# The last half tile in two pieces, late stores on ScalarE's queue, and a new order of work

## Chip, cores and metric

The kernel runs on one core of a Trainium2 chip. The metric is the device time of one execution in microseconds (us). A core has TensorE (PE, matrix products, with its weight loads as PEld), VectorE (DVE), ScalarE (ACT), GpSimd (POOL) and SyncE (SP), which here only issues DMAs. Each of the five runs its own list of instructions in order; semaphores join them.

## What is computed

A gate g, one number for each of the 2048 tokens, mixes two attention layers over the same x (640 wide, 32 heads of 20): A is linear attention with softmax feature maps, B is causal attention inside four segments of 512 tokens, with a memory carried from segment to segment.

```python
g = _sigmoid((x * gate_w).sum(-1, keepdims=True))
# A: phi = softmax(+-(q @ w_phi)) and the same for k, 40 wide
kv = einsum('bhsf,bhsd->bhfd', phi_k, v);  z = einsum('bhsf->bhf', phi_k)
a = (einsum('bhqf,bhfd->bhqd', phi_q, kv) / (phi_q . z + 1e-6)) @ wo_A
# B: for each segment s of 4
p = softmax(q_s @ k_s.T * 20**-0.5 + mask)
o = sigmoid(beta) * (phi(q_s) @ M) / (phi(q_s) @ z) + (1 - sigmoid(beta)) * (p @ v_s)
M += phi(k_s).T @ v_s;  z += phi(k_s).sum()
b = o @ wo_B
return g * a + (1 - g) * b
```

## The kernel before

The kernel is a list of 1394 operations, built in `build` (L1019). An operation is one step of one engine (a chain of matmuls, one evacuation, one DMA) with the tiles that it reads and writes. `Graph.replay` then takes three texts that stand in the file: ORDER, the place of every operation in one list (each engine runs its own operations in that order, SP's DMAs too); ENGINE, for the 255 operations that two or three engines could do, which of them does it; and PLACE, the buffer or the PSUM banks of each of the 618 floating tiles. `emit` adds the semaphore waits that follow from the tiles: data, and the reuse of a buffer or bank. At the very end SP waits for every DMA slot whose landing it doesn't know of yet (L253).

The steps that the prediction speaks of, by their lines:

- Setup: weights are loaded and turned or cast (WB, L499, on DVE, ACT or POOL), x is turned on PE (L484), and the first segment is projected (qproj0 L593, kproj0 L604) and copied out as qk (q0_ev, k0_ev). The two weight products with w_phi are made on PE (fuse, L567) and copied out as WkA and WqA. The last of those and all evacuations below go through `evac` (ACT L426 or DVE L427).
- B, for each segment: projections (L613 for q and k, L633 and L634 for v); QK bursts (L730), four heads side by side, into two PSUM tiles of two banks; each tile goes through one exp on ACT (L741, 160 exps of 128x1024 in all), is masked on POOL (L743) and used by the PV step (L773), whose result nT is copied out and written to memory; `b_out` reads it back as nB, divides (nrec L806, nmul L808), and adds the memory's part aT (nadd, L717).
- B's memory: k and q pass through a feature map (pk, pq: L652 to L654), Mmm (L671) and mr (L702) are its products, L708 to L711 its evacuation.
- A: pkA and vA (L818), kexp (L831), sums and scaling (L837 to L841), kv (L861) with its sums (L874, L884); then for each 512 tokens pqA (L931), qexp (L938), ssum (L946), the scaling of half of ET by sp (Esc, L962), and for each tile of 128 tokens U (L976) with its evacuation (L982 to L985).
- The end: `final(t)`, for each of 16 tiles of 128 tokens. Two PE steps (final0 from A's oTA, final1 from B's nB; L1006) add ten products into two PSUM banks of 320 columns; an evacuation scales them by 1-g, and a store writes 128x640. For the last four tiles each half of 320 columns has its own two steps, evacuation and store. All stores of results go through SP.

PE, ACT, DVE and POOL thus work on A, B and final interleaved, as ORDER says. PSUM has 8 banks; S and U and F tiles take two each.

Of the kernel before, what the change touches and what calls it, by code (L numbers as in the profile page):

```python
# [16 lines left out]
NT = 16  # L17
# [244 lines left out]
class GatedMix(Graph):  # L262
# [730 lines left out]
    def final(self, t):  # L993
        pt = self.pst("F", 2)
        ob = self.sbt("out", [128, D], BF16, self.p_out)
        oT, nB, q = self.oTA[t], self.nB[t // 4], t % 4
        parts = ((0,), (1,)) if t >= NT - 4 else ((0, 1),)
        ops = {}
        for bs in parts:
            for k, (lhs, R) in enumerate(((lambda c: oT[:, c, :], [(oT, "*"), (self.Wo, 0)]),  # L1000
                                          (lambda c: nB[:, c, 128 * q:128 * q + 128], [(nB, q)] + [(self.Wo, (1, dd)) for dd in range(4)]))):
                def mm(e, k=k, lhs=lhs, bs=bs):
                    first = ops[bs, k].pos < ops[bs, 1 - k].pos
                    for c in range(NCH):
                        for b in bs:
                            r = e.matmul(self.pf(pt, b, 0, 320), lhsT=lhs(c), rhs=self.Wo[:, NCH * k + c, 320 * b:320 * b + 320],  # L1006
                                         start=(first and c == 0), stop=(not first and c == 4), skip_group_check=True)
                    return r
                ops[bs, k] = self.op("pe", f"final{k}", mm, R=R, W=[(pt, (bs[0], k))])
        out2d = self.out.rearrange("b s d -> (b s) d")  # L1010
        for bs in parts:
            n, c0 = len(bs), 320 * bs[0]
            src = (lambda: self.pbanks(pt, 320)) if n == 2 else (lambda b=bs[0]: self.pf(pt, b, 0, 320))
            dst = (lambda: ob[:, :].rearrange("p (b c) -> p b c", b=2)) if n == 2 else (lambda c0=c0: ob[:, c0:c0 + 320])
            self.evac("out_ev" if n == 2 else "outh_ev", dst, src, R=[(self.omg, t // 4)],
                      W=[(pt, (bs[0], 0)), (pt, (bs[0], 1)), (ob, bs[0])], scale=lambda: self.omg[:, t:t + 1])
            self.dma("sp", "out", out2d[128 * t:128 * (t + 1), c0:c0 + 320 * n], lambda c0=c0, n=n: ob[:, c0:c0 + 320 * n], R=[(ob, bs[0])])
# [140 lines left out]
```

## Time and profile before

| | us |
|---|---|
| median of 3 runs (lowest, highest) | 289.42 (289.36, 290.12) |
| the profiled execution, device time | 288.96 |
| its span, first to last instruction | 287.2 |
| mean granted TensorE clock in it | 1.000 |
| PE, DVE, ACT, POOL busy | 275.4, 224.1, 234.5, 163.7 |

The page gives busy time of each engine, a picture of the span in 40 slices, DMA queues, the chain of waits that ended last, and the costliest groups of instructions. Busy time of PE is that of overlapping matmuls: one of 320 columns is shown with 299 ns, while the next starts 136 ns later. An instruction that waits is not busy; the time is put down to what came last.

### The profile page before, as it was taken

To read this page: it belongs to the slowest core of one execution; us is meant where nothing else is said; L and a number is where in the kernel's file an instruction comes from. 1 tells how busy PE (TensorE), PEld (TensorE's weight loads), DVE (VectorE), ACT (ScalarE), POOL (GpSimd) and SP (SyncE) were. 2 spreads that over 40 slices of the span, in tenths; PEclk is the share of its full clock that TensorE was granted. 3 is DMA by queue.
4 is the path that set the end of the run, shared out by engine and by line. 5 is a ranking of instruction groups with operands and counts; after the bars stand their busy time and mean duration, and the time that the engine had idled before them with its cause. 6 is when DMAs were issued, how large, how long until landed. Compare 5 with 4: busy or idle time off the path is not lost.

```text
span 287.2 us, 7648 instructions
## 1 busy us (share of the span) xinstructions
PE 275.4 (96%) x3155; PEld 162.2 (56%) x3155; DVE 224.1 (78%) x395; ACT 234.5 (82%) x270; POOL 163.7 (57%) x171
## 2 busy tenths in 40 slices
PE   7999999999999899999999999989998999999996
PEld 3755535564356555646754554544465456667774
DVE  3777997856896799988799979787963696788873
ACT  3589999898999998899799999999899988772110
POOL 6421698638869648796794671584955434263030
PEclk9999999999999999999999999999999999999999
DMA  7999400551158046432135664985946596665793
GB/s 227 259 249 227 91 21 18 114 77 37 57 92 126 14 112 132 59 84 75 34 41 103 161 154 101 188 231 121 154 107 160 120 215 184 151 146 145 168 182 113
DMA packets 75212, 36.25 MB, mean 126 GB/s; under 512 B 56458, under 2 KB 73258, under 8 KB 75178
## 3 DMA queue, kind: packets, MB, share of 16 engines
q1 hardware_dynamic: 73872, 34.26, 54.0%
q10 hardware_dynamic: 1242, 1.48, 1.5%
q8 instruction: 25, 0.41, 0.6%
q0 software_dynamic: 64, 0.03, 0.1%
q14 instruction: 9, 0.07, 0.1%
HBM read 13.44 MB, written 11.50 MB: 87 GB/s over the span
## 4 chain that ended last, share of the span: by engine, by line
PE 68%; ACT 18%; DVE 7%; POOL 5%; issue 1%; POOLq 0%
PE ps L1006 14%; PE ps L818 9%; PE ps L613 9%; ACT exA L741 9%; PE ps L730 6%; PE ps L773 5%; PE ps L931 5%; ACT exC L741 4%; PE ps L861 3%; PE ps L976 3%; PE ps L633 3%; PE ps L634 2%; ACT ET L938 2%; DVE z L837 2%; PE ps L604 2%; PE ps L593 2%
## 5 line engine op out<-in xcount | busy, mean ns | idle before, releaser
L741 ACT ACTIVATE exA<-ps 128x1024 bf16<-128x1024 f32 x128 | 123.4, 1034 | 12.4 <-PE ps L730 12.1
L743 POOL TENSOR_SCALAR_AFFINE_SELECT exA<-exA 128x1024 bf16<-128x1024 bf16 (+1 forms) x64 | 58.1, 917 | 55.9 <-ACT exA L741 55.9
L841 POOL TENSOR_TENSOR E<-E,z 128x640 bf16<-128x640 bf16 x26 | 34.2, 1325 | 10.2 <-DVE lc L637 7.6
L613 PE MATMUL ps<-xT,WB 128*128 128x512 bf16 x150 | 37.0, 380 | 1.1 <-ACT exA L741 0.8
L741 ACT ACTIVATE exC<-ps 128x1024 bf16<-128x1024 f32 x32 | 31.0, 1023 | 4.1 <-PE ps L730 3.8
L730 PE MATMUL ps<-qk 20*128 20x128 bf16 (+3 forms) x512 | 31.7, 301 | 1.9 <-ACT exA L741 0.8
L831 ACT ACTIVATE E<-ps,sg 128x640 bf16<-128x640 f32 x32 | 25.3, 803 | 1.0 <-DVE acc L884 0.4
L743 POOL TENSOR_SCALAR_AFFINE_SELECT exC<-exC 128x1024 bf16<-128x1024 bf16 x16 | 18.4, 1153 | 12.3 <-ACT exC L741 12.3
L818 PE MATMUL ps<-WvA,xT 128*128 128x320 bf16 x160 | 24.1, 300 | 0.8 <-ACT exA L741 0.8
L837 DVE TENSOR_REDUCE z<-E 128x64 f32<-128x1280 bf16 x16 | 23.5, 1471 | 1.5 <-ACT E L831 1.4
L931 PE MATMUL ps<-xT,WqA 128*128 128x512 bf16 x100 | 24.1, 380 | 0.5 <-ACT exC L741 0.3
L818 PE MATMUL ps<-WkA,xT 128*128 128x320 bf16 x160 | 24.1, 300 | 0.3 <-ACT exC L741 0.3
L1006 PE MATMUL ps<-Wo,oTA 128*128 128x320 bf16 x160 | 24.4, 299 | 0.0
L1006 PE MATMUL ps<-Wo,nB 128*128 128x320 bf16 x160 | 24.2, 299 | 0.0
L427 DVE CAST nT<-ps 128x512 bf16<-128x512 f32 x25 | 16.6, 682 | 8.8 <-PE ps L773 8.8
L427 DVE CAST qk<-ps 128x1024 bf16<-128x1024 f32 (+1 forms) x17 | 17.4, 1032 | 7.4 <-PE ps L613 5.3
L773 PE MATMUL ps<-exA,v1B 128*32 128x384 bf16 (+2 forms) x384 | 22.7, 311 | 0.2 <-POOL exA L743 0.2
L633 PE MATMUL ps<-WvB,xT 128*128 128x320 bf16 x80 | 22.5, 300 | 0.2
L613 PEld LDWEIGHTS ps<-xT,WB 128*128 128x128 bf16 x150 | 12.9, 98 | 17.3 <-issue 2.7
L884 POOL TENSOR_TENSOR acc<-acc,E 128x640 bf16<-128x640 bf16 x13 | 18.1, 1395 | 7.8 <-DVE acc L884 6.7
L634 PE MATMUL ps<-WvB,xT 128*128 128x321 bf16 x80 | 22.4, 300 | 0.0
L730 PEld LDWEIGHTS ps<-qk 20*128 20x128 bf16 x512 | 9.1, 92 | 23.6 <-issue 7.6
(132 smaller groups left out, 497.4 us busy)
## 6 DMA issues: line engine op xcount, KB each, us to landing
scn<-nT SPq DMA_DIRECT2D x32, 128.0 KB, 1.8
scq<-rr SPq DMA_DIRECT2D x16, 160.0 KB, 3.0
sp<-scq SPq DMA_DIRECT2D x4, 640.0 KB, 4.4
scr<-qk SPq DMA_DIRECT2D x16, 120.0 KB
qk<-scr SPq DMA_DIRECT2D x16, 120.0 KB
nB<-scn SPq DMA_DIRECT2D x12, 160.0 KB, 3.5
out_dram<-out SPq DMA_DIRECT2D x12, 160.0 KB, 2.1
stk<-in_B_wk_dram SPq DMA_DIRECT2D x5, 160.0 KB, 5.1
```

Of the source, the lines that this page charges most:

```text
L427: return e.tensor_scalar(o(), i(), scale(), None, op0=ALU.mult) if scale else e.tensor_copy(o(), i())
L613: r = e.matmul(self.pf(pt, w, 0, LSEG), lhsT=WB[:, w, kc, 128 * c:128 * (c + 1)], rhs=xT[:, kc, LSEG * n:LSEG * (n + 1)], start=(kc == 0), ...
L633: e.matmul(self.pf(pt, 0, 0, 320), lhsT=l, rhs=self.WvB[:, kc, 0:320], start=(kc == 0), stop=(kc == 4))
L730: r = e.matmul(self.pf(pts[i // 2], i % 2, c0, N), lhsT=qk[32 * i:32 * i + DH, g, 1, 128 * j:128 * (j + 1)], rhs=qk[32 * i:32 * i + DH, g, ...
L741: self.op("act", "exp", lambda e, p=p: e.activation(view(p), self.pbanks(pts[p], 512), ACT.Exp, scale=scale), W=[(pts[p], 0), (t, (key, p))])
L743: self.op("pool", "mask" + str(len(pat)), lambda e: e.affine_select(mv(), mv(), pattern=pat, compare_op=ALU.is_ge, fill=0.0, base=0, chann ...
L773: r = e.matmul(self.ps[32 * i:32 * i + 32, 512 * pt.t[0] + 128 * j:512 * pt.t[0] + 512], lhsT=vt[:, v0:v0 + 32], rhs=src(j, i), start=(j = ...
L818: r = e.matmul(self.pf(pt, b, 0, 320), lhsT=l, rhs=W[:, kc, 320 * b:320 * b + 320], start=(kc == 0), stop=(kc == 4))
L837: self.op("dve", "Zred", lambda e: e.tensor_reduce(z[:, :, :].rearrange("p s h -> p (s h)"), E[:, :, :].rearrange("p s (h d) -> p (s h) d" ...
L841: self.op(("pool", "dve"), "Anorm", lambda e, s=s: e.tensor_tensor(Ev(s), Ev(s), z[:, s, :].rearrange("p (h o) -> p h o", o=1).to_broadcas ...
L931: r = e.matmul(self.pf(pt, k, 0, LSEG), lhsT=self.WqA[:, kc, 128 * c:128 * (c + 1)], rhs=xT[:, kc, LSEG * S:LSEG * (S + 1)], start=(kc == ...
L1006: r = e.matmul(self.pf(pt, b, 0, 320), lhsT=lhs(c), rhs=self.Wo[:, NCH * k + c, 320 * b:320 * b + 320], start=(first and c == 0), stop=(no ...
```

## The change

In `final`, the last four tiles (`late`) issue their stores on ACT's queue in place of SP's. The very last tile's second half becomes two pieces of 160 columns with two PE steps, an evacuation and a store each; the second piece has a PSUM tile of one bank of its own. So four operations and one tile are added (1398 and 619). ORDER, ENGINE and PLACE are new texts throughout. 60 of the operations of before that have a choice of engine run on another one.

```diff
-        parts = ((0,), (1,)) if t >= NT - 4 else ((0, 1),)
+        late = t >= NT - 4
+
+        parts = [(pt, (0, 1), 320, 0)] if not late else [(pt, (0,), 320, 0)] + (
+            [(pt, (1,), 320, 320)] if t < NT - 1 else [(pt, (1,), 160, 320), (self.pst("F", 1), (0,), 160, 480)])
...
+        for pt, bs, n, d0 in parts:
...
-                        for b in bs:
-                            r = e.matmul(self.pf(pt, b, 0, 320), lhsT=lhs(c), rhs=self.Wo[:, NCH * k + c, 320 * b:320 * b + 320],
+                        for i, b in enumerate(bs):
+                            r = e.matmul(self.pf(pt, b, 0, n), lhsT=lhs(c), rhs=self.Wo[:, NCH * k + c, d0 + 320 * i:d0 + 320 * i + n],
...
-            self.dma("sp", "out", out2d[128 * t:128 * (t + 1), c0:c0 + 320 * n], lambda c0=c0, n=n: ob[:, c0:c0 + 320 * n], R=[(ob, bs[0])])
+            self.dma("act" if late else "sp", "out", out2d[128 * t:128 * (t + 1), d0:d0 + w], lambda d0=d0, w=w: ob[:, d0:d0 + w], R=[(ob, d0)])
```

The end of ORDER names the last operations. In the numbers of `final(15)` before, 1386 and 1387 are the PE steps of the first half, 1388 and 1389 those of the second, 1390 to 1393 the evacuations and stores. After, 1386 and 1387 are the first half's, 1388 and 1389 the first piece's, 1390 and 1391 the second piece's; 1392 and 1393, 1394 and 1395, 1396 and 1397 are the evacuations and stores of the three.

```diff
-1363 1364 1372 1329 902 1380 1366 1378 1367 1373 1376 1377 1370 1371 1381 1384 1385 914 1374 1375 1353 1365 1368 1369 1387 1379 1382 1383 1386 1390
-1391 1389 1388 1392 1393
+1364 1368 1379 1325 1380 1369 1378 1381 1384 1366 1385 1382 1352 1383 1353 1372 1373 1376 1377 1357 1361 887 1367 1390 914 1370 1371 1374 1375 1391
+1396 1397 1389 1388 1394 1395 1386 1387 1392 1393
```

Operations by engine, where it changed most (before, after): Anorm POOL 26, 21 and DVE 6, 11; chain DVE 18, 15 and POOL 13, 16; WB ACT 5, 8 and DVE 12, 8; q0_ev ACT 1, 4; fuse_ev ACT 3, 5; nT_ev ACT 7, 8; qk_ev ACT 4, 5; vA_ev ACT 6, 5; out_ev ACT 5, 7; nadd POOL 3, 6; nmul POOL 0, 1; Esc of one chunk POOL 0, 3.

## Rows read from the trace of the kernel before

**Rows 1.** The page's busy shares, and its chain of waits by engine.

```profile
PE 275.4 (96%) x3155; PEld 162.2 (56%) x3155; DVE 224.1 (78%) x395; ACT 234.5 (82%) x270; POOL 163.7 (57%) x171
PE 68%; ACT 18%; DVE 7%; POOL 5%; issue 1%; POOLq 0%
```

**Rows 2.** The chain of waits in order of time: start us, us, what.

```profile
71.94 1.08 PE ps L613 x5
...
85.75 2.89 PE ps L818 x20
...
89.92 0.33 PE ps L730 x8
...
101.16 0.66 PE ps L773 x16
...
202.84 1.25 PE ps L931 x5
...
213.18 0.36 PE ps L730 x8
...
215.50 5.50 ACT exA L741 x6
...
252.87 0.80 PE ps L976 x12
...
262.41 0.69 PE ps L976 x12
...
266.90 17.67 PE ps L1006 x130
284.59 0.53 ACT out L426
```

**Rows 3.** The first instructions in order of time: start us, us, engine, line, what.

```profile
0.81 0.41 ACTq L418 DMA_DIRECT2D xn<-in_A_x_dram  x1
0.81 0.39 SPq L418 DMA_DIRECT2D xn<-in_A_x_dram  x1
...
1.26 3.57 PE L466 MATMUL ps<-zero 128*128 128x512 bf16 x8 [1.26 <-DVE sg L514]
```

**Rows 4.** Busy time by stretch: length, then each engine's us (instructions), clock, DMA.

```profile
95.00:102.50 7.50, 6.85 (x154) 4.69 (x155) 6.42 (x11) 7.42 (x9) 3.69 (x4) 1.00 0.18 46
213.30:221.00 7.70, 6.89 (x66) 3.75 (x59) 3.21 (x8) 7.44 (x9) 2.15 (x2) 1.00 0.52 122
...
257.80:284.60 26.80, 26.76 (x264) 19.80 (x260) 19.90 (x41) 4.08 (x8) 5.76 (x5) 1.00 0.68 159
284.60:287.20 2.60, 0.00 (x0) 0.00 (x0) 0.00 (x0) 0.52 (x1) 0.00 (x0) 1.00 0.20 63
```

**Rows 5.** Groups of instructions of the last 33 us: count, busy us, mean ns.

```profile
L1006 PEld LDWEIGHTS ps<-Wo,nB 128*128 128x128 bf16 x90 | 8.6, 98 | 3.4 <-issue 0.2
```

**Rows 6.** The end in order of time, all engines; idle time before in brackets.

```profile
281.95 3.53 SPq L418 DMA_DIRECT2D out_dram<-out  x5
...
284.59 0.53 ACT L426 ACTIVATE out<-ps,omg 128x320 bf16<-128x320 f32 x1 [5.58 <-PE ps L1006]
```

**Rows 7.** DMA issues: count, KB each, median us from issue to landing.

```profile
out_dram<-out SPq DMA_DIRECT2D x8, 80.0 KB, 1.7
```

**Rows 8.** Groups of ACT, shapes apart: count, busy us, mean ns, idle before.

```profile
L426 ACT ACTIVATE nT<-ps 128x512 bf16<-128x512 f32 x7 | 4.3, 619 | 2.9 <-PE ps L773 2.9
L426 ACT ACTIVATE vA<-ps 128x640 bf16<-128x640 f32 x6 | 4.2, 706 | 0.3 <-PE ps L818 0.2
L426 ACT ACTIVATE qk<-ps 128x1024 bf16<-128x1024 f32 x4 | 4.1, 1033 | 0.3 <-PE ps L613 0.3
...
L426 ACT ACTIVATE WkA<-ps 128x640 bf16<-128x640 f32 x3 | 2.1, 706 | 0.4 <-PE ps L567 0.2
...
L499 ACT ACTIVATE WB<-stk 128x240 bf16<-128x240 bf16 x2 | 0.7, 395 | 1.5 <-DMA stk<-in_B_wk_dram 1.5
```

**Rows 9.** Who waited for whom: us in total, times, longest us.

```profile
PEld ps L730 <- DVE nT L427: 1.6, 3, 0.8
...
PEld ps L730 <- DVE out L427: 0.9, 1, 0.9
PEld ps L976 <- POOL ET L962: 0.9, 1, 0.9
...
PEld ps L861 <- DVE vA L427: 0.9, 1, 0.9
```

More of the change, by code (lines that the diff above doesn't have):

```diff
@@ L996, in final @@
         oT, nB, q = self.oTA[t], self.nB[t // 4], t % 4
-        parts = ((0,), (1,)) if t >= NT - 4 else ((0, 1),)
+        late = t >= NT - 4
+        parts = [(pt, (0, 1), 320, 0)] if not late else [(pt, (0,), 320, 0)] + (
+            [(pt, (1,), 320, 320)] if t < NT - 1 else [(pt, (1,), 160, 320), (self.pst("F", 1), (0,), 160, 480)])
         ops = {}
-        for bs in parts:
+        for pt, bs, n, d0 in parts:
             for k, (lhs, R) in enumerate(((lambda c: oT[:, c, :], [(oT, "*"), (self.Wo, 0)]),
@@ L1001, in final, with mm @@
                                           (lambda c: nB[:, c, 128 * q:128 * q + 128], [(nB, q)] + [(self.Wo, (1, dd)) for dd in range(4)]))):
-                def mm(e, k=k, lhs=lhs, bs=bs):
-                    first = ops[bs, k].pos < ops[bs, 1 - k].pos
+                def mm(e, k=k, lhs=lhs, pt=pt, bs=bs, n=n, d0=d0):
+                    first = ops[d0, k].pos < ops[d0, 1 - k].pos
                     for c in range(NCH):
-                        for b in bs:
-                            r = e.matmul(self.pf(pt, b, 0, 320), lhsT=lhs(c), rhs=self.Wo[:, NCH * k + c, 320 * b:320 * b + 320],
+                        for i, b in enumerate(bs):
+                            r = e.matmul(self.pf(pt, b, 0, n), lhsT=lhs(c), rhs=self.Wo[:, NCH * k + c, d0 + 320 * i:d0 + 320 * i + n],
@@ L1007, in mm @@
                                          start=(first and c == 0), stop=(not first and c == 4), skip_group_check=True)
                     return r
-                ops[bs, k] = self.op("pe", f"final{k}", mm, R=R, W=[(pt, (bs[0], k))])
+                ops[d0, k] = self.op("pe", f"final{k}", mm, R=R, W=[(pt, (bs[0], k))])
         out2d = self.out.rearrange("b s d -> (b s) d")
[L1011 to L1016, printed above, removed]
-            self.dma("sp", "out", out2d[128 * t:128 * (t + 1), c0:c0 + 320 * n], lambda c0=c0, n=n: ob[:, c0:c0 + 320 * n], R=[(ob, bs[0])])
+        for pt, bs, n, d0 in parts:
+            w = n * len(bs)
+            src = (lambda pt=pt: self.pbanks(pt, 320)) if len(bs) == 2 else (lambda pt=pt, b=bs[0], n=n: self.pf(pt, b, 0, n))
+            dst = (lambda: ob[:, :].rearrange("p (b c) -> p b c", b=2)) if len(bs) == 2 else (lambda d0=d0, n=n: ob[:, d0:d0 + n])
+            self.evac("out_ev" if len(bs) == 2 else "outh_ev" if n == 320 else "outq_ev", dst, src, R=[(self.omg, t // 4)],
+                      W=[(pt, (bs[0], 0)), (pt, (bs[0], 1)), (ob, d0)], scale=lambda: self.omg[:, t:t + 1])
+            self.dma("act" if late else "sp", "out", out2d[128 * t:128 * (t + 1), d0:d0 + w], lambda d0=d0, w=w: ob[:, d0:d0 + w], R=[(ob, d0)])
@@ L1047 @@
 ORDER = """
[40 rows of a table removed]
[40 rows of a table added]
 """
 ENGINE = "".join("""
-010002000000110210000121111000111111110111001011111101111111111111111111111110100110000101101111101110010010010011010110111111100000001010001001001000
-011100101111111001001001001001100001000110010010011000111100000000001001110011000001010111110000111101110
+011000010011121101202102110100111100100001101011111101111101011111111111111100100110010000111111101110010000111111010110111111001010001001101001011011
+1101010101110110010110010001111001100000110110011110000100011110000001011100111011001100111010000100110011
 """.split())
 PLACE = """
[11 rows of a table removed]
[11 rows of a table added]
 """
```

98 rows, old and new, of tables (ORDER, PLACE) are left out of this document.

## The prediction

> **What bounds the kernel now.** I read the page's busy shares first, then the chain of waits, then the stretches, then the waits themselves. TensorE (PE) looks full: 96% busy, with ScalarE (ACT) at 82% [rows 1]. But matmuls are pipelined, so a busy PE can still be behind another engine; the chain of waits puts 18% of the span on ACT [rows 1]. To see how much time PE really loses, I priced every PE step of the order list by its back-to-back time in the chain [rows 2]: ten 320-column matmuls 1.36 to 1.45 us, five 512-column ones 1.08 to 1.25, a QK burst of eight 0.33 to 0.36, a PV step of sixteen 0.66, a U step of twelve 0.69 to 0.80. Over the whole list that is 266.3 us. From PE's start at 1.3 us [rows 3] to its end at 284.6 there are 283.3 us, so PE loses about 17 us, in many small pieces. After its end come 0.53 us of ACT [rows 2] and the last store.
>
> Three parts are seen in the stretches [rows 4]. Until 28.7 us, the end of the 8th exp, the engines fill up. From there to 257.8 us, when the last exp ends, PE and ACT share the bound: the exps need ACT, and PE must refill the PSUM tiles that ACT empties. Behind 257.8 us PE is busy 26.76 of 26.8 us, ACT 4.08. The last 2.6 us hold only one ACT step and the store.
>
> To see which engine holds a stretch up I cut the list after every 8th of the 160 exps and added up PE's and ACT's work between two cuts (an exp in a row of them at 0.92 us, 5.50 us for six [rows 2]). The larger of the two sums gives the measured length within 0.3 us in 11 of the 19 stretches behind the first. Two stretches are plainly ACT's: exps 57 to 64 (95.0 to 102.5 us) have 3.7 us of PE work against 7.5 of ACT work and took 7.5; exps 129 to 136 (213.3 to 221.0 us) have 3.7 against 7.5 and took 7.7 [rows 4]. PE fell 3.8 us behind in each, and the stretch after each was 2.0 and 2.7 us shorter than its larger sum, since some of its PE steps had started early: some 2.9 us stayed lost.
>
> **The change, part by part.**
>
> *The split.* The last tile's right half becomes two pieces of 160 columns: 20 matmuls of 160 columns for 10 of 320. The nearest row is U's twelve of mostly 147 columns, 0.80 us or 67 ns each [rows 2]; in proportion 160 columns take 73 ns, 20 of them 1.45 us, against 1.36 for the ten. Bounds: nothing (half of 136 ns each) and +0.6 us (each paced by its weight load, 98 ns [rows 5], 1.96 us). I take +0.1, since U's step has the same form. But the new order does not put the pieces last: it ends with the two steps of the other half (320 columns), its evacuation by ACT and its store. So the end is again one evacuation of 320 columns, 0.53 us [rows 6], and the narrower evacuations, by VectorE (DVE), lie under the last 1.36 us of PE. The split saves nothing at the end.
>
> *Stores on ACT's queue.* Nine stores leave SyncE's (SP) queue for ACT's. Issuing the same load takes 0.41 us on ACT's queue and 0.39 on SP's [rows 3]. Nine are 3.7 us of ACT, and each waits in ACT's own order for its evacuation, DVE's too; behind it stand the next evacuations. In the last 26.8 us ACT is busy only 4.1 [rows 4], which covers it. I walked the new list's end with these durations: the store ahead of the final evacuation is issued some 0.6 us before PE's last matmul ends, and PSUM bank 6, which the split takes, was left by tile 12 over three microseconds before. Without that cover each store would cost its 0.41 us. The last store waits for ACT itself instead of for a handover to SP: between -0.1 and +0.2 us, and I take 0. From the last evacuation's end (285.12 [rows 6]) to the span's end (287.2) there are 2.08 us, of which a half tile's store takes 1.7 to land [rows 7]; the other 0.4 is the end of SP's list, which waits in turn for the slot of every store. With a second queue there are more slots to wait for, and the store that lands last need not be the last one waited for: 0 to +0.4, and I take +0.2.
>
> SP's last five stores are issued within 3.53 us [rows 6], so its queue is free when the last one comes. The Trainium skill (DMA: Bandwidth & Descriptors, Issuing engines are not separate DMA queues) says that DMAs run on the same 16 DMA engines whichever engine starts them, and that starting them on several saves only the issue time. By that rule the moved stores give nothing at the end, and the sum stays as it is; if a queue of its own let the last store land sooner, it would be by SP's issue, about 0.4 us at most.
>
> *The new order.* Work behind the last exp is the same, 26.0 us of PE against 26.6, and I find no late operand there (the nearest, the last tile's nB, is ready some 2.5 us before its matmul). So what counts is how much PE loses before. ACT gets 4.9 us more work before its last exp (249.4 to 254.3 by the rows' prices): 3.2 of it in the setup (eight more casts and copies of 0.4 to 0.7 us, two given back [rows 8]), where PE's work of 23.2 us in the stretch of the first eight exps covers ACT's 20.8; the other 1.7 later (two nT, one qk, one out, less vA and KVa [rows 8]). Of the 1.7 between 0 and all isn't covered. With the same cuts, ACT's excess over PE sums to 13.3 us before and 13.7 after; averaged over shifted and longer cuts the two lists' sums differ by between -2.6 and +0.8 us. The two bad stretches are better (9.1 and 6.1 us of PE work against 7.5), others worse: exps 25 to 32 have 6.0 against 8.2, exps 65 to 72 have 9.9 against 12.6. I take +0.5.
>
> Waits for DVE and GpSimd (POOL) get looser. PE's longest single wait in the middle, 0.9 us, is U's for POOL's scaling of ET [rows 9]: the list now has 1.4 us of PE work between the two where it had 0.4, so it goes; the kv step's wait for DVE's vA [rows 9] gets 0.33 us between. Between a mask and its PV stand 4.1 us of PE work in the median case, 2.5 before. I take -1.2 (the first whole, 0.3 of the second). Bounds: -3.5, the four longest such waits gone (0.9, 0.9, 0.9 and 0.8 [rows 9]), and 0, if something else is late then.
>
> *The sum:* +0.1 + 0 + 0.2 + 0.5 - 1.2 = -0.4 us. Against the profiled execution's 288.96 us (span 287.2 and 1.8 around it) that is 288.6; the median of the runs is 0.46 above that execution, so the forecast for the median is 289.0.
>
> **The rivals.**
> *The evened stretches pay in full.* If PE's new work at exps 57 to 64 and 129 to 136 removes the 2.9 us that stayed lost, and the newly thin stretches are made good by their neighbours, the order's ACT part is -2.0 or so in place of +0.5: 286.5 to 286.9, taken as 286.9. For it: in both places PE sits in gaps between exps with nothing else late. Against it: ACT's total excess isn't smaller.
>
> *ACT falls behind at exps 65 to 80 (slower).* There the new list has 20.6 us of PE work against 24.8 of ACT's, 4.2 short over sixteen exps; before, PE had 25.0 against 23.5. PE has 2.6 us too much in the sixteen exps ahead (21.0 against 18.4). If PE can't spread that, because the PSUM tiles are held, over 1.3 us net is enough to make it slower than before; with 2.9 us lost for the 0.5 of the sum, 289.0 + 2.4 gives 291.4. Against it: in the stretches measured, more than half of such a loss came back.
>
> *The change does not do what it says.* The pieces aren't at the end and the moved stores save no time there; with an order worth nothing either way the time is 289.4 to 289.7.
>
> **How the numbers follow.** The forecast has 0.42 (0.14 of it faster by over 0.3%, 0.26 level, 0.02 slower); the evened stretches 0.25, all faster; ACT behind 0.27, all slower; nothing gained 0.06, level. So 0.39 faster, 0.32 within 0.3% (0.9 us, about what a measurement of this kernel tells from no change), 0.29 slower. Cases of both signs hold most of the chance: the forecast's own range is 287.9 to 290.1. For 8 in 10 the range reaches down to 286.4, half a microsecond under the first rival, and up to 291.6, just over the second; the unknown terms, -3.5 to 0 for DVE and POOL and -2.6 to +1.7 for ACT, make it so wide.
>
> **What would show it.** The last PE work should run on end as now, the last ACT step take 0.53 us, and from its end to the span's end there should be 2.0 to 2.5 us: under 1.9 would prove the stores' part wrong, as would a PE wait for ACT among the final steps. At exps 57 to 64 PE should be busy over 7 us, with more projections. No 0.9 us wait of U for POOL should be left. If the time is off by more than 2 us, the exps between which the two profiles drift apart tell which rival it was: 65 to 80 for the slower one.

## The result, and the profile after

The changed kernel takes 292.31 us (median of 6 runs, 291.78 to 294.0) where the kernel before takes 289.46 (6 runs beside it). The ratio is 1.010 with a 95% interval of 1.0073 to 1.0127: slower, by 2.9 us. The forecast was 289.0 with 286.4 to 291.6; the result lies outside the range, and the time moved the other way. Some executions of either kernel have a mean granted clock of 0.993 or 0.994 and take some 2 us longer; medians here are of all executions, while the ratios leave out the slowest of those.

The profiled execution took 292.38 us, its span is 290.4 us: 3.2 us more than the span of before, and 0.2 us more around it (1.98 against 1.76). The page's span, busy shares and chain by engine answer to [rows 1]:

```profile
span 290.4 us, 7678 instructions
PE 275.9 (95%) x3165; PEld 163.3 (56%) x3165; DVE 219.9 (76%) x383; ACT 238.7 (82%) x280; POOL 170.2 (59%) x174
PE 60%; ACT 25%; DMA 7%; DVE 4%; SPq 2%; issue 1%; POOL 1%; DVEq 0%
```

PE works 0.5 us more, in a span 3.2 us longer, so the time went into waiting; and the chain of waits by engine (last line), where DMAs had no share worth a line, now has 7% of them and 2% of SP's issues. To see where, I read the ends of the same exps in both traces; the two lists swap neighbours, but up to each place of the table the same exps have run in both:

| end of | before, us | after, us | apart |
|---|---|---|---|
| 8th exp | 28.7 | 30.6 | +1.9 |
| 64th | 102.5 | 104.2 | +1.7 |
| 80th | 128.2 | 130.2 | +2.0 |
| 88th | 147.6 | 147.5 | -0.1 |
| 96th | 157.7 | 159.4 | +1.7 |
| 128th | 213.3 | 214.6 | +1.3 |
| 160th, the last | 257.8 | 259.8 | +2.0 |
| PE's last matmul | 284.6 | 287.3 | +2.7 |
| the span | 287.2 | 290.4 | +3.2 |

So +1.9 us came ahead of the 8th exp, nothing in the 152 exps behind it (2.0 us are won once and lost again), +0.7 in the steps behind the last exp, +0.5 behind PE's end. The rows of these three places follow.

**The start.** PE's first instructions of after, with the idle time before a group in brackets; they answer to [rows 3]:

```profile
1.40 2.74 PE L466 MATMUL ps<-zero 128*128 128x512 bf16 x6 [1.40 <-DVE zero L460]
...
15.56 1.25 PE L604 MATMUL ps<-xT,WB 128*128 128x512 bf16 x5
18.56 0.79 PE L567 MATMUL ps<-BD,wkT 128*128 128x140 bf16 x12 [1.74 <-DMA wkT<-in_A_wqkv_dram]
19.19 1.24 PE L604 MATMUL ps<-xT,WB 128*128 128x512 bf16 x5
```

PE stands 1.74 us for wkT, the key weights of A, which SP loads with a transposing DMA. The chain of waits has it as one piece, from its issue at 5.52 us to 18.43 (start, us, what):

```profile
5.52 12.91 DMA wkT<-in_A_wqkv_dram
```

Before, PE's first fuse step (L567) began at 17.17 us and waited for nothing; wkT had landed at 16.7. The same transfer, issued at the same time, landed 1.7 us later. What changed around it is ScalarE's load of WvB (800 KB), issued at 7.9 us in place of 9.35. The DMA issues of after (count, KB, median us from issue to landing):

```profile
WvB<-in_B_wv_dram ACTq DMA_DIRECT2D x1, 800.0 KB, 10.5
```

Before, that load took 7.1 us. Issued 1.5 us earlier, it landed 2 us later, at 18.4, with wkT.

**Behind the last exp.** The same stretches as in [rows 4]: exps 57 to 64, exps 129 to 136, the last exp to PE's end, and the tail (us, then each engine's busy us, clock, DMA share, GB/s):

```profile
96.70:104.20 7.50, 6.92 (x154) 4.71 (x155) 7.40 (x11) 7.42 (x9) 4.09 (x5) 1.00 0.03 11
214.60:222.20 7.60, 6.73 (x73) 3.98 (x66) 6.77 (x14) 7.39 (x9) 2.80 (x3) 1.00 0.82 157
259.80:287.30 27.50, 26.47 (x262) 19.28 (x258) 17.09 (x36) 5.38 (x10) 6.61 (x5) 1.00 0.68 169
287.30:290.40 3.10, 0.00 (x0) 0.00 (x0) 0.00 (x0) 0.52 (x1) 0.00 (x0) 0.99 0.14 40
```

In the third line PE has 1 us of idle time where it had 0.04. Its two waits, and what SP issues ahead of them, in order of time:

```profile
263.12 0.45 SPq L418 DMA_DIRECT2D out_dram<-out  x1
263.61 2.19 SPq L418 DMA_DIRECT2D scn<-nT  x1
265.85 1.21 SPq L414 DMA_TRANSPOSE oTA<-oA  x1
267.37 1.77 SPq L418 DMA_DIRECT2D nB<-scn  x4
...
268.55 0.84 PE L1009 MATMUL ps<-Wo,oTA 128*128 128x320 bf16 x5 [0.33 <-DMA oTA<-oA]
...
275.47 1.80 PE L1009 MATMUL ps<-Wo,nB 128*128 128x320 bf16 x12 [0.65 <-DVE nB L717]
```

The chain of waits runs through the same place (start, us, what); it answers to the last lines of [rows 2], where 17.67 us of PE stood in one piece:

```profile
263.61 3.74 DMA scn<-nT
...
268.70 4.69 DMA nB<-scn
...
273.41 0.96 DVE nB L806
...
274.39 0.50 DVE nB L808
...
274.92 0.50 DVE nB L717
...
275.47 11.80 PE ps L1009 x95
...
287.29 0.53 ACT out L426
```
The last write of nT to memory is issued at 263.61, behind two stores of results that the new order puts ahead of it on SP, and its issue alone takes 2.19 us. The read nB follows at 267.37, DVE gets it at 273.41, and PE waits 0.65 us for the sum at 275.47. Before, the read was issued at 263.96 and DVE began at 269.30; PE's steps ran on end from 257.8 to 284.6.

**The end**, which answers to [rows 6]; PE, DVE, ACT and its queue:

```profile
282.95 1.19 PE L1009 MATMUL ps<-Wo,oTA 128*128 128x160 bf16 x10
...
285.24 0.39 DVE L427 TENSOR_SCALAR out<-ps,omg 128x160 bf16<-128x160 f32 x1 [0.61 <-PE ps L1009]
285.41 1.33 ACTq L418 DMA_DIRECT2D out_dram<-out  x3
287.29 0.53 ACT L426 ACTIVATE out<-ps,omg 128x320 bf16<-128x320 f32 x1 [1.91 <-PE ps L1009]
287.85 0.34 ACTq L418 DMA_DIRECT2D out_dram<-out  x1
```

The last store is issued on ACT's queue at 287.85 and has landed by 289.48. SP then still goes through eight waits for semaphores that have long been raised, one about every 62 ns, from 289.55 to 289.98, before its list ends. Before, the landing of the last store released SP's last wait, and the list ended 0.1 us later. From ACT's last evacuation to the span's end it is now 2.58 us; it was 2.08.

### The profile page after: what moved, and what is told of

It is laid out like the page before. It is cut to its first block, busy times and chain, and to the rows that moved or that the text cites. A ratio compares the mean times of both kernels' runs of the same rounds, so it can differ in the third digit from the quotient of the medians.

```text
span 290.4 us, 7678 instructions
## 1 busy us (share of the span) xinstructions
PE 275.9 (95%) x3165; PEld 163.3 (56%) x3165; DVE 219.9 (76%) x383; ACT 238.7 (82%) x280; POOL 170.2 (59%) x174
## 4 chain that ended last, share of the span: by engine, by line
PE 60%; ACT 25%; DMA 7%; DVE 4%; SPq 2%; issue 1%; POOL 1%; DVEq 0%
ACT exA L741 14%; PE ps L818 10%; PE ps L1009 10%; PE ps L613 9%; PE ps L730 6%; PE ps L931 5%; PE ps L773 5%; DMA wkT<-in_A_wqkv_dram 4%; PE ps L861 3%; ACT E L831 3%; ACT exC L741 3%; PE ps L976 2%; PE ps L633 2%; PE ps L634 2%; SPq L418 2%; PE ps L671 2%
## 5 line engine op out<-in xcount | busy, mean ns | idle before, releaser
L741 ACT ACTIVATE exA<-ps 128x1024 bf16<-128x1024 f32 x128 | 124.2, 1034 | 13.1 <-PE ps L730 11.8
L743 POOL TENSOR_SCALAR_AFFINE_SELECT exA<-exA 128x1024 bf16<-128x1024 bf16 (+1 forms) x64 | 60.7, 958 | 53.6 <-ACT exA L741 53.2
L730 PE MATMUL ps<-qk 20*128 20x128 bf16 (+3 forms) x512 | 31.7, 300 | 2.3 <-ACT exA L741 1.7
L841 POOL TENSOR_TENSOR E<-E,z 128x640 bf16<-128x640 bf16 x21 | 28.6, 1372 | 4.1 <-DVE z L839 4.0
L743 POOL TENSOR_SCALAR_AFFINE_SELECT exC<-exC 128x1024 bf16<-128x1024 bf16 x16 | 18.2, 1138 | 18.4 <-ACT exC L741 18.4
L1009 PE MATMUL ps<-Wo,nB 128*128 128x320 bf16 (+1 forms) x165 | 24.5, 295 | 0.6 <-DVE nB L717 0.6
L884 POOL TENSOR_TENSOR acc<-acc,E 128x640 bf16<-128x640 bf16 x16 | 23.2, 1452 | 2.6 <-DVE acc L884 2.1
L1009 PE MATMUL ps<-Wo,oTA 128*128 128x320 bf16 (+1 forms) x165 | 24.4, 295 | 0.3 <-DMA oTA<-oA 0.3
L426 ACT ACTIVATE out<-ps,omg 128x640 bf16<-128x640 f32 (+1 forms) x11 | 7.7, 698 | 20.2 <-PE ps L1009 19.7
L773 PE MATMUL ps<-exA,v1B 128*32 128x384 bf16 (+2 forms) x384 | 22.0, 311 | 0.3 <-POOL exA L743 0.2
L938 ACT ACTIVATE ET<-ps 128x1024 bf16<-128x1024 f32 (+1 forms) x24 | 20.9, 910 | 0.2
```

Source lines behind the costliest of these rows:

```text
L730: r = e.matmul(self.pf(pts[i // 2], i % 2, c0, N), lhsT=qk[32 * i:32 * i + DH, g, 1, 128 * j:128 * (j + 1)], rhs=qk[32 * i:32 * i + DH, g, ...
L741: self.op("act", "exp", lambda e, p=p: e.activation(view(p), self.pbanks(pts[p], 512), ACT.Exp, scale=scale), W=[(pts[p], 0), (t, (key, p))])
L743: self.op("pool", "mask" + str(len(pat)), lambda e: e.affine_select(mv(), mv(), pattern=pat, compare_op=ALU.is_ge, fill=0.0, base=0, chann ...
L773: r = e.matmul(self.ps[32 * i:32 * i + 32, 512 * pt.t[0] + 128 * j:512 * pt.t[0] + 512], lhsT=vt[:, v0:v0 + 32], rhs=src(j, i), start=(j = ...
L841: self.op(("pool", "dve"), "Anorm", lambda e, s=s: e.tensor_tensor(Ev(s), Ev(s), z[:, s, :].rearrange("p (h o) -> p h o", o=1).to_broadcas ...
L1009: r = e.matmul(self.pf(pt, b, 0, n), lhsT=lhs(c), rhs=self.Wo[:, NCH * k + c, d0 + 320 * i:d0 + 320 * i + n], start=(first and c == 0), st ...
```

## The experiments

My theory after the two traces: the middle of the new order is level, and the loss is three mishaps at its rims, (a) WvB's early load delays wkT, (b) stores ahead of the nT write on SP delay nB, (c) the second queue leaves SP waits behind the last landing. Rivals: PE's fuse step stands too early in the list (for a), the pieces of 160 columns are to blame (for c), and the new order costs something of its own in the middle. All results in one table; the ratio is to the kernel before, run beside it on the same chip.

| kernel | median, us | before, us | ratio (95%) |
|---|---|---|---|
| the changed kernel | 292.31 | 289.46 | 1.0100 (1.0073 to 1.0127) |
| a1_fuse_behind | 294.10 | 289.80 | 1.0156 (1.0120 to 1.0192) |
| a2_wvb_later | 290.90 | 289.80 | 1.0046 (1.0024 to 1.0068) |
| a3_stores_on_sp | 291.90 | 289.80 | 1.0064 (1.0041 to 1.0087) |
| a4_stores_behind | 292.61 | 289.80 | 1.0102 (1.0071 to 1.0133) |
| b1_wvb_early | 291.52 | 289.66 | 1.0064 (1.0030 to 1.0098) |
| b2_act_stores | 290.30 | 289.66 | 1.0015 (0.9993 to 1.0036) |
| c1_three_together | 290.43 | 289.66 | 1.0032 (1.0004 to 1.0059) |
| c2_waits_sorted | 293.05 | 289.66 | 1.0087 (1.0059 to 1.0116) |
| b3_split_at_end | 289.84 | 289.50 | 1.0020 (0.9995 to 1.0046) |
| b4_split_act_sorted | 289.39 | 289.50 | 0.9998 (0.9974 to 1.0022) |
| b5_wvb_later | 289.77 | 289.50 | 1.0012 (0.9988 to 1.0037) |
| e1_u_later | 289.32 | 289.75 | 0.9978 (0.9955 to 1.0001) |
| e2_u_later_split | 289.24 | 289.75 | 0.9981 (0.9954 to 1.0008) |

Kernels a and c start from the changed kernel, b and e from the kernel before. In the diffs the numbers are operations of ORDER.

### The start: fuse later, or WvB later

```diff
 a1: kproj0 (169, 171) and their copies ahead of the first fuse steps
-101 219 102 138 139 130 103 118 115 116 169 166 132 ... 135 171 172 170
+101 219 102 169 166 171 172 138 139 130 103 118 115 116 132 ... 135 170
 a2: ACT's load of WvB (14) two of ACT's copies later (52, 54)
-32 153 14 154 52 56 54 155
+32 153 154 52 56 54 14 155
```

> The changed kernel with one thing undone: in ORDER the kproj0 steps 169 and 171 (and their copies 166, 172) stand ahead of the first fuse step 138 again, as in the kernel before. Nothing else moves. Theory: PE stands still for 1.7 us at 16.9 us because the fuse steps, moved ahead of two kproj0 steps, need wkT, which lands only at 18.4 us; the loss is carried to the end (the 8th exp ends 1.9 us late, the last one 2.0). Then this gains 1.2 to 1.6 us: 290.7 to 291.1, and PE's wait for wkT shrinks to under 0.6 us. Rival 1: the time lost there would be lost later anyway, since ACT holds the middle; then 292.0 to 292.4 with the wait gone. Rival 2 (that the ACT part of the new order is what costs): the same, 292 or more.

> The changed kernel with ACT's load of WvB (800 KB) issued behind two more casts, at about 9.3 us as in the kernel before, in place of 7.9 us. PE's order is left as changed. Theory: wkT lands 1.7 us later than before because WvB's packets share the DMA engines with it from earlier on. Then wkT lands at about 16.7 us, PE's wait goes and the time falls by 1.3 to 1.7 us: 290.6 to 291.0. Rival: wkT is late for another reason (the second x transpose, which the new list issues right behind the first); then it lands at 18.4 as now and the time stays at 292.0 to 292.5.

a1 was a miss. PE no longer waits for wkT, but it is later still (the 8th exp ends at 31.7 us): the fuse steps now come so late that their own copies are late. PE of a1:

```profile
17.53 2.33 PE L604 MATMUL ps<-xT,WB 128*128 128x512 bf16 x10 [0.43 <-ACT qk L426]
19.70 0.79 PE L567 MATMUL ps<-BD,wkT 128*128 128x140 bf16 x12
21.38 1.12 PE L567 MATMUL ps<-BD,wkT 128*128 128x140 bf16 x18 [0.89 <-DVE WkA L427]
22.98 0.39 PE L730 MATMUL ps<-qk 20*128 20x512 bf16 x4 [0.48 <-ACT WkA L426]
```

Moving the reader back is no remedy. a2 is one: with WvB issued at 9.0 us it takes 6.7 us to land, wkT lands at 15.9, the fuse step starts at 17.14 without a wait and the 8th exp ends at 29.2. It gives back 1.4 us at the last exp (258.4 against 259.8), 1.6 us of 2.9 by the ratios. (In a2's profile PE also waits 1.35 us for an x tile at 7.2 us, a wait that the changed kernel's profile doesn't have.)

### The same load, early and late, in the kernel before

```diff
 b1: WvB (14) behind ACT's first copy
-75 50 16 44 ... 18 51 14 82
+75 50 14 16 44 ... 18 51 82
 b5: WvB one copy later
-18 51 14 82 54 83 84 56 60 57
+18 51 82 54 83 84 56 60 14 57
```

> The kernel before with one thing moved: ScalarE issues the 800 KB load of WvB right behind its first copy WB1 instead of behind the third WB0 copy and gw, so at about 8 us instead of 9.35 us; every other instruction keeps its place. Theory (the early load takes transfer time from the transposing load wkT, which the first K projections need): wkT lands 1 to 2 us later than 16.6 us, the eighth exp ends 1 to 2 us later than 28.7, and the median is 290.5 to 291.5 us where the kernel before has 289.5. Rival (the load is harmless in itself, and the changed kernel lost its start because its PE puts the first fuse step ahead of the first K projection): wkT lands within 0.4 us of 16.6 and the time stays within 0.5 us of the kernel before.

> The kernel before with ScalarE's load of WvB one copy later, behind the wait of that copy for the stored weights, so issued at about 11.4 us instead of 9.35 us. Theory (how early WvB is issued sets when the transposing load wkT lands, and in the kernel before wkT lands 0.5 us ahead of its first reader): wkT lands earlier than 16.7 us, and the time doesn't move, 289.4 to 289.9 us, since nothing waited for it; WvB lands by 18.5 us, ahead of its reader at 20.8. Rival (any earlier landing shortens the start): 289.0 us or less.

b1 carries the loss over into the kernel before, with nothing else changed. Its median is 1.9 us above that of the kernel before. Among executions with a mean clock of 1.00 alone the difference is 1.0 us (290.58, 7 of 12, against 289.63, 31 of 34); the rest comes from the five executions of b1 at 0.994. The delay is larger than I expected at the landing, 19.75 us, and comes with a second wait, 0.88 us for POOL's Mk. PE of b1:

```profile
13.59 2.32 PE L604 MATMUL ps<-xT,WB 128*128 128x512 bf16 x10 [0.88 <-POOL Mk L504]
...
19.89 0.79 PE L567 MATMUL ps<-BD,wkT 128*128 128x140 bf16 x12 [1.39 <-DMA wkT<-in_A_wqkv_dram]
```

b5's time came as expected, but not for the reason given: wkT did not land earlier but at 17.6 us, and its reader started at 17.96 instead of 17.17. So "the later WvB, the earlier wkT" is wrong. What the 15 traces show is a place in time. In the order of WvB's issue:

| kernel | WvB issued, us | WvB, issue to landing | wkT landed, us |
|---|---|---|---|
| b1 | 7.6 | 11.8 | 19.75 |
| a1, a4 | 7.7 | 10.2, 10.9 | 18.1, 18.9 |
| a3 | 7.8 | 11.8 | 19.8 |
| after | 7.9 | 10.5 | 18.4 |
| c2 | 8.0 | 9.4 | 17.7 |
| e2 | 8.9 | 7.6 | 16.7 |
| a2, c1 | 9.0, 9.1 | 6.7, 6.5 | 15.9, 15.9 |
| before, b4, b2, b3 | 9.35 to 9.65 | 6.2 to 7.3 | 15.8 to 17.1 |
| e1 | 10.2 | 6.3 | 16.7 |
| b5 | 12.1 | 5.3 | 17.6 |

All issues up to 8.0 us gave a landing at 17.7 or later, all from 8.9 to 10.2 one at 17.1 or earlier. Both transfers get slower together in the early cases, so it isn't that WvB merely takes wkT's share. The DMA packets in the traces show what differs. WvB is 640 packets of 1280 bytes on ACT's queue (q10), wkT 3200 of 256 bytes on SP's (q1), 800 KB each. The 2.5 us from 13.3 to 15.8 us, before and then after (packets, MB, share of 16 engines):

```profile
q10 hardware_dynamic: 666, 0.82, 98.0%
q1 hardware_dynamic: 256, 0.06, 10.8%
...
q10 hardware_dynamic: 252, 0.32, 80.3%
q1 hardware_dynamic: 667, 0.17, 36.7%
```

Whenever WvB was issued, its packets start to move between 12.4 and 14.6 us. In the nine kernels with an issue from 8.9 us on, at least 3144 of wkT's 3200 packets had started by then, and WvB's 640 took 2.2 to 2.5 us. In the six with an issue up to 8.0 us, 2468 to 2914 had; the rest mixed with WvB's, and WvB's took 4.0 to 4.8 us. In all 15 the landing of wkT comes 0.8 to 1.1 us after WvB's last packet, even in the kernel before, where wkT's own last packet had moved by 13.6 us. b5 fits this: there WvB's packets ended at 16.7 us, in the kernel before at 15.7. Why an earlier issue mixes the two, and why mixed packets are slower, the runs don't show.

### The end: stores and closing waits

```diff
 a3: all stores on SP
-            self.dma("act" if late else "sp", "out", ...
+            self.dma("sp", "out", ...
 b2: the kernel before, the last four tiles' stores on ACT
-            self.dma("sp", "out", ...
+            self.dma("act" if t >= NT - 4 else "sp", "out", ...
 c2 (and b4, e2): SP's closing waits in the order of the last operation on each semaphore
-        for k, s in allsem.items():
+        final = {o.key: o.pos for o in self.order if o.key is not None}
+        for k, s in sorted(allsem.items(), key=lambda i: final.get(i[0], -1)):
 a4: the stores of t5 and t6 (1337, 1341) behind the reads of nB (876 to 879) on SP
-862 1337 863 ... 874 1341 875 ... 726 876 1345
+862 863 ... 874 875 ... 726 876 1337 1341 1345
```

> The changed kernel with the nine late stores back on SP's queue, everything else as changed, the two pieces too. Theory: from the end of the last evacuation to the span's end there were 2.08 us before and 2.58 after, because SP goes through eight more waits (for ACT's slots and its own) once the last store has landed. Then the tail is 2.1 us again and the time falls by 0.4 to 0.5 us: 291.8 to 291.9. Rival: a store from ACT's queue itself lands later, or the late stores on ACT save something that this gives back; then it stays at 292.3 or rises.

> The kernel before with the stores of the last four tiles (eight halves of 320 columns) issued by ScalarE instead of SP; orders, pieces and everything else as before. Theory (SP's closing waits go through the slots of each queue in a fixed order, and ScalarE's queue with nine slots in use comes after SP's or has waits left behind the last landing): the tail from PE's end to the end of the span goes from 2.6 to about 3.1 us, and the median is about 290.0 us, 0.5 above the kernel before. Rival (the tail of the changed kernel grew because of its two pieces of 160 columns, not because of the queue): the time stays within 0.2 us of the kernel before.

> The changed kernel with SP's closing waits put in the order in which the last operation on each semaphore stands in the program, so that the wait for the last store comes last; the stores stay on ScalarE's queue, nothing else changes. Theory (0.5 us of the tail is eight waits of about 64 ns each that come behind the one for the last landing): the tail from PE's end to the end of the span goes from 3.1 to about 2.6 us and the median from 292.3 to 291.8 us. Rival (the tail is longer because a store issued by ScalarE lands later or is reported later): the tail stays at 3.1 us, the time at 292.3.

> The changed kernel with SP's stores of tiles 5 and 6 (1337, 1341) behind the reads of nB (876 to 879) in place of ahead of the last two writes of nT. Theory: these 160 KB stores stand in SP's queue ahead of the last write of nT, whose issue took 2.19 us and whose landing came 3.7 us after its issue; nB is read late, so nrec starts 11.9 us after the last PV step (8.7 before), and PE waits 0.5 us for oTA and 0.8 us for nB among the final steps. Then nrec starts 1 to 2 us earlier, both waits go, and the time falls by 0.8 to 1.3 us: 291.0 to 291.5. Rival: the last write of nT is late because DVE copies nT late; then nrec stays where it is and the time at 292.3.

PE's end is where ACT's last evacuation starts; from there to the span's end:

| | before | after | a2 | a3 | b2 | c1 | c2 | b3 | b4 |
|---|---|---|---|---|---|---|---|---|---|
| last evacuation starts, us | 284.59 | 287.29 | 285.78 | 291.00 | 286.79 | 287.34 | 287.72 | 285.25 | 284.83 |
| span, us | 287.2 | 290.4 | 288.9 | 293.7 | 290.0 | 290.0 | 290.4 | 287.7 | 287.2 |
| tail, us | 2.6 | 3.1 | 3.1 | 2.7 | 3.2 | 2.7 | 2.7 | 2.5 | 2.4 |

The tail is 3.1 to 3.2 us in each kernel with late stores on ACT and the old closing waits, 2.4 to 2.7 in each without one of the two. a3 takes the queue away, b2 adds it to the kernel before without the pieces (+0.6 us, where I expected 0.5), and c2 keeps queue and pieces and only sorts the waits. So (c) is the order of SP's closing waits; the queue and the pieces are not slower themselves. In whole times the half microsecond is at the edge of what can be seen: a3 and b2 point to it; c2's ratio is 0.4 us under the changed kernel's (1.0087 against 1.0100), well inside the intervals. The profiled execution of a3 is 3.9 us above its median (the clock fell in it, see the last section) and is used for its tail alone.

a4 did only in part what it should: the nT writes are issued in 1.05 us for two, and nB's wait is gone from PE, but DVE starts on nB 12.8 us after the last exp, against 13.6 in the changed kernel and 11.5 before, 0.8 us earlier where I had expected 1 to 2. PE and DVE of a4, where the sum is there at 275.20 and the PE step, at 275.84, has no wait:

```profile
273.12 2.88 PE L1009 MATMUL ps<-Wo,oTA 128*128 128x320 bf16 x20
...
274.71 0.49 DVE L717 TENSOR_TENSOR nB<-nB,aT 128x640 bf16<-128x640 bf16 x1
...
275.84 2.34 PE L1009 MATMUL ps<-Wo,nB 128*128 128x320 bf16 x16
```

But from the last exp to PE's end it is still 27.2 us (27.4 after, 26.7 before), and the median of 292.61 shows no gain over the changed kernel. PE now waits elsewhere in the stretch: 0.42 us at 264.22 for DVE's copy of nT. c1 below, which has a4's edit too, waits 0.80 us there and takes 27.4 us, as long as the changed kernel:

```profile
263.92 1.53 PE L1009 MATMUL ps<-Wo,nB 128*128 128x320 bf16 x10 [0.80 <-DVE nT L427]
```

So nB's wait of 0.65 us was worth 0.2 us at most in the stretch. All seven traces of the new order have 0.5 to 1.4 us of PE waits there, all eight of the old order none: (b) names one late operand of several, and moving the two stores does not repair the place. For the total a4 is inconclusive, since wkT came later still in it (18.9 us).

### The three together

```diff
 c1: the edits of a2, a3 and a4 in one kernel
```

> The changed kernel with three things put back at once: ScalarE's load of WvB four copies later (issue at about 9.3 us instead of 7.9), all stores on SP's queue, and the stores of the tiles t5 and t6 behind the reads nr on SP. The searched order of everything else stays. Theory (these three places are the whole loss, and the middle of the new order is level with the old one): 1.4 + 0.5 + 0.3 us off 292.3, so 289.8 to 290.2 us, within 0.3% of the kernel before. Rival (the new order costs something of its own in the stretches of the exps as well): it stays at or above 290.7 us.

290.43 us lies between the two expectations, nearer the theory's 290.2 than the rival's 290.7; the ratio of 1.0032 leaves 0.1 to 1.7 us. By medians of the spans (the time without what lies around it) it is 288.4 us against 288.0 of the kernel before, so in the span 0.4 us is left. The other 0.4 us lies outside the span: 2.1 us there in c1 and a3, 1.9 to 2.0 in the other kernels with the new order, 1.7 in all with the old one, b3 and b4 with their added operations and pieces included. What makes it I can't tell from the traces, which show only the span. So what c1 gets back is the first place (1.6 us by a2's ratio) and the third (0.5 us of tail). The second is still there in its trace (27.4 us behind the last exp, 26.7 before), and the new order, so repaired, is still no better than the old.

### The split alone, and the diff's code on the old order

```diff
 b3: pieces put last in ORDER, all stores on SP        b4: the same, stores on ACT, closing waits sorted
-... 1387 ... 1386 1390 1391 1389 1388 1392 1393
+... 1387 ... 1386 1392 1393 1389 1388 1394 1395 1391 1390 1396 1397
```

> The kernel before with the split alone, and with the two pieces really at the end: the second half of t15 becomes ten matmuls of 160 columns, VectorE's copy and a store, then ten more, ScalarE's copy and a store; all stores on SP's queue, every other instruction in its old place. Theory (my costing of the split): the ten additional matmuls and weight loads cost PE 0.1 us or a little more, the shorter last copy (0.4 against 0.53 us) and the shorter store give 0.1 to 0.2 back, so 289.5 to 289.8 us where the kernel before has 289.65, and the time outside the span stays at 1.7 us. Rival (the additional store on SP lengthens the end, because SP issues it 0.4 us behind the other): 290.0 us or more.

> The same as the kernel with the split at the end, with the stores of the last four tiles on ScalarE's queue as the change has it, and with SP's closing waits in the order in which the last operation on each semaphore stands in the program. Theory (the tail grew by waits behind the last landing alone, and those are now ahead of it): the same time as with the split on SP's queue within 0.2 us, 289.4 to 289.8 us. Rival (ScalarE's queue is slower at the end for a reason of its own): at least 0.4 us above it.

PE and ACT of b3 at the end:

```profile
283.66 0.51 PE L1009 MATMUL ps<-Wo,nB 128*128 128x160 bf16 x5
284.01 0.51 PE L1009 MATMUL ps<-Wo,oTA 128*128 128x160 bf16 x5
284.36 0.51 PE L1009 MATMUL ps<-Wo,nB 128*128 128x160 bf16 x5
284.70 0.51 PE L1009 MATMUL ps<-Wo,oTA 128*128 128x160 bf16 x5
285.25 0.39 ACT L426 ACTIVATE out<-ps,omg 128x160 bf16<-128x160 f32 x1 [5.61 <-PE ps L1009]
```

Five matmuls of 160 columns start 0.345 us after the five before, 69 ns each; 20 take 1.38 us against 1.36 for the ten. The last evacuation is 0.39 us instead of 0.53. Both times are level with the kernel before: 289.84 is 0.04 above the upper end of what I expected of b3, 289.39 at the lower end for b4. I had expected b4 within 0.2 us of b3 and it is 0.45 lower, a difference inside their intervals; the rival, at least 0.4 above, is out. So ACT's queue costs nothing in b4. The code of the diff, with its pieces really at the end and the waits sorted, is worth nothing that can be measured; what hurt was the order searched for it, and SP's waits behind the last landing, which the second queue brought.

### One wait taken away alone

The prediction's largest term was PE's 0.93 us wait of U for POOL. In the changed kernel it was gone: POOL is done with ET at 192.47, U starts at 193.17 behind 0.20 us of wait for an exp of ACT; and no gain was to be seen.

```diff
 e1 (on before) and e2 (on b4): U (1178) behind the next projection (745)
-728 729 1178 664 730 731 638 745 669
+728 729 664 730 731 638 745 1178 669
```

> The kernel before with one PE step moved: the U step that waits 0.93 us for GpSimd's ET at 191.7 us comes behind the next Q/K projection (five 512-column matmuls, 1.25 us) instead of ahead of it. Theory one (the prediction's term: time that PE loses in such a wait comes off the end): the wait goes, everything behind is 0.7 to 0.9 us earlier, the last exp ends at 257.0 instead of 257.8 and the median is 288.7 to 288.9 where the kernel before has 289.6. Theory two (PE's and ScalarE's sums set the length of these stretches, and PE waits for an exp a little later instead): at the end of the exps at most 0.2 us is left of it, the median stays within 0.3 us of the kernel before.

> The kernel with the split at the end, the late stores on ScalarE's queue and SP's closing waits sorted, with the same U step moved behind the next projection. Theory one: 0.7 to 0.9 us below that kernel's 289.4, so 288.5 to 288.7 us, faster than both kernels. Theory two: 289.1 to 289.5 us.

PE of e2:

```profile
191.43 1.25 PE L614 MATMUL ps<-xT,WB 128*128 128x512 bf16 x5 [0.36 <-DVE aM L712]
192.52 0.85 PE L977 MATMUL ps<-KV,ET 128*128 128x147 bf16 x12
193.31 0.40 PE L731 MATMUL ps<-qk 20*128 20x128 bf16 x8
193.64 2.58 PE L614 MATMUL ps<-xT,WB 128*128 128x512 bf16 x10
196.16 0.40 PE L731 MATMUL ps<-qk 20*128 20x512 bf16 x4
...
200.46 0.73 PE L977 MATMUL ps<-KV,ET 128*128 128x147 bf16 x10 [0.26 <-DVE oA L986]
```

U's wait is gone, but the projection now waits 0.36 us for DVE. Ahead of this place e2 was 0.09 us later than the kernel before; the QK burst starts 0.31 us earlier than before (193.31 against 193.62), so 0.4 of the 0.93 us were won here. The next burst is 0.05 us ahead (196.16 against 196.21), and so is the U step at 200.46: two thirds of that was given back within 3 us. Theory two holds in the traces: from the 8th to the last exp it is 229.0 us in e1 and e2, 229.1 in the kernel before, and 228.9 in b4, without the move. The medians, 0.4 and 0.5 us under the kernel before, are just above the 0.3 us that it leaves and under the 0.7 to 0.9 of theory one; both intervals reach 1. e2 has the lowest median of all, 289.24 us, but it can't be told from the kernel before.

## Why the prediction was wrong

- *"PE's work of 23.2 us in the stretch of the first eight exps covers ACT's 20.8"*: this step failed. It weighed the added casts against PE in sums and asked whether ACT had time. What mattered was ACT's DMA of WvB: 11 of ACT's steps stand ahead of it in either list, but others, and it was issued 1.5 us earlier. The prediction counted DMAs in ACT's list at the end only and put the start's loads at nothing. Cost: +1.9 us in the profile, of which a2 gets back 1.4 at the last exp; b1 shows the same delay of wkT with nothing else changed.
- *"I find no late operand there"*: this failed too. nB was to be ready 2.5 us before its matmul; PE waited 0.65 us for it (and 0.33 for an oTA). The only issue times that it gives are of some 0.4 us [rows 3]; the nT write behind two stores took 2.19 us to issue. The stretch is 0.7 us longer, of which a4 shows 0.2 as nB's and c1 none; with nB's wait gone PE waits for DVE's copy of nT. What the other 0.5 hang on, one by one, is open.
- *SP's closing waits, +0.2 (0 to +0.4)*: right in its mechanism and mis-sized: +0.5 (a3, b2, c2). The upper bound took the 0.4 us seen before; the eight waits behind the landing are additional to it.
- *The new order's ACT part, +0.5, and the waits for DVE and POOL, -1.2*: by the table of exps these together gave +0.1 between the 8th and the last exp. The wait of U for POOL went as said; that it would come off the end was wrong (e1, e2). The two bad stretches took 7.5 and 7.6 us, 7.5 and 7.7 before, and PE was busy 6.92 us at exps 57 to 64, not over 7 [rows 4].
- *The split, +0.1*: right; 69 ns each, and level in b3. *The moved stores, 0*: right, with the waits sorted (b4). The sentence from the Trainium skill (DMA: Bandwidth & Descriptors, Issuing engines are not separate DMA queues) that the prediction draws on agrees with b4, where ACT's queue gives no gain beyond the noise (289.39 us beside b3's 289.84), and with b1, where a load on ACT's queue delays one on SP's (wkT at 19.75 us for 16.7).
- *The slower rival, ACT behind at exps 65 to 80*: right in sign only. These sixteen exps took 26.0 us against 25.7; its price was 2.4. The outcome was in none of the cases: all put the loss where PE and ACT share the bound, and none at the rims, where a few single transfers decide.
- Outside the span the changed kernel has 0.2 us more; no step had it, and its cause is open.

## What to carry to other kernels

Where a new order is weighed, a balance of the engines' sums says little about start and end: list there, for each first reader of a loaded tile, when its load is issued, what other loads are then in flight, and how much slack is left (wkT had 0.5 us). A DMA that is issued earlier isn't free because the engine has time; the cheapest test is to move it alone in the kernel that worked. And a wait's length is the upper bound of what removing it gives: look at what the same engine waits for next.

## What I had not expected of the hardware

- A DMA issue instruction can itself become long: 2.19 us for an nT write behind two stores on SP's queue, where the same form took 0.43 us two places earlier.
- A load issued earlier can land later in absolute time: WvB issued at 7.6 to 8.0 us landed between 17.4 and 19.6, issued at 9.0 to 9.65 between 15.5 and 16.9.
- A wait can cost twice. In b2's profiled execution PE waited 1.3 us for DVE at 191 us, shortly after 0.5 us for ACT (0.56 us of matmuls lie between), and then the granted clock was 0.50, the lower of its two levels (1.2 of 2.4 GHz), from 192.0 to 195.4 us. b2 by stretch (PE first, granted clock third from the end):

```profile
190.00:191.00 1.00, 0.00 (x0) 0.00 (x0) 1.00 (x1) 1.00 (x2) 1.00 (x1) 1.00 1.11 332
191.00:192.00 1.00, 0.74 (x18) 0.47 (x19) 0.93 (x5) 0.16 (x1) 1.00 (x2) 1.00 1.28 287
192.00:193.00 1.00, 1.00 (x15) 1.00 (x16) 0.71 (x2) 0.96 (x2) 1.00 (x2) 0.51 1.26 283
```

That execution took 291.75 us, 1.5 above its kernel's median. The waits of 1.74 us in the changed kernel at 18.6 us and of 2.33 us in a4 at 19.0 us left the clock at 1.00, so the length of one wait alone does not decide it. In a3's, where PE waited 3.2 us for wkT, the clock was 0.50 from 21.2 to 24.7 us.
- At the start PE can run at half pace where the views print a granted clock of 1.00. In c1's profiled execution (1.7 us above its median) five matmuls of 256 columns took 1.27 us, where those of the kernel before took 1.27 us for ten, at the same place. c1's trace holds clock records only from 10.7 us on (the kernel before from 4.7), and 1.00 is printed where there is none:

```profile
7.49 1.27 PE L593 MATMUL ps<-xT,WB 128*128 128x256 bf16 x5
```
